# Re-timing the opening of a filter, routing and expert kernel: third batch, DRAM writes, filter rows and weight conversions

## The chip, the cores and the metric

The kernel runs on one core of one Trainium2 chip. Its engines are called as in the profile: PE is TensorE (PEld its weight loads), DVE is VectorE, ACT is ScalarE, POOL is GpSimd, and SP is SyncE, which issues transfers. The metric is the time of one execution on the device in microseconds (us). The clock that the throttle granted to TensorE is written as a share of full speed.

## What is computed

```python
X = np.fft.rfft(x, axis=1)                      # x: 8 batches x 3072 x 256
y = np.fft.irfft(X * (filt_r + 1j*filt_i), n=3072, axis=1)
x = y.reshape(8*3072, 256)
logits = x @ w_gate                             # 8 experts
e = argmax(logits); gate = softmax(logits)[e]
# each token goes to its expert e in order, until `capacity` (768) rows are taken
h = relu(disp @ w1)                             # per expert: 768x256 @ 256x1024
out[token] = gate * (h @ w2)                    # 1024x256; tokens without a place: 0
h = out @ w_in                                  # 256x2048
g = softplus(h)
result = g @ w_out                              # 2048x256
```

The 8 x 768 places are full after three batches, so the common path filters and routes batches b0, b1 and b2 alone. All other rows of the output are one constant row.

## The kernel before

The work falls into units of 384 rows of one expert, 16 units in all: eight leading ones, which take the first 384 places of each expert, and eight later ones.

**Filter.** A batch's 3072 points are taken as 96 x 32. `x1` (b0) and `x1_out` (b1, b2) are the first transform. Those of b1 and b2 are written to DRAM (`mid`, line 223) and read back turned (`it`, `load_i`), eight writes of 384 KB for each of the two batches. `s2(b, k)`, k = 0 to 11, is the second transform (L236) with the complex filter behind it: four DVE multiplies over 64 partitions each (L240, L245, L246, L248; five where k is 0) and one add (L249), on POOL for b0 and for even k, on DVE for odd k. `s3` (L260, copy `e` L262) goes back, then `tr2` (L268, copy `j` L271) and `s4` (L305, copy `yt` L306) make the filtered rows.

**Routing.** `gsum` (L283) and `gturn` (L296) make the logits once all twelve `s3` of a batch are through, `gate` (L313 to L366, some twenty small DVE instructions in five pieces) the places; its last result that routing waits for is `tk` (L365). Then POOL scatters the batch's rows by 32 indirect transfers (L382), at most three per step. Rows of b2 are only parked (`park`, line 393, eight writes issued by SP). Unit 0 may load its rows (`xd`, L532) when the scatters of b0, b1 have landed.

**Experts and the last layers.** `load_w` and `split_w` fetch w1 and w2 and split each into a high and a low part (`w1h`, `w2h` on ACT, L411; `w1l`, `w2l` on POOL, L412). `w1` (L563; `hh` on ACT L567, `hl` on DVE L568) and `w2` (L580) are the experts. `wi` (L595) and `wo` (L618) are the last two layers.

**Conversions.** w_in and w_out come as 64-bit floats, 32 pieces of 128x256. `split_res` turns each into a high and a low part by five DVE instructions (`wtop` L470, `wr` L472, `wrf` L474, `whb` L481, `wtop` again L483), three on ACT (`wrf` L475, `whb` L478, high part L486) and one on POOL (low part L484). It is a generator: `convert`, called once a step, moves every piece in work one stage further, and starts a new one if `new` is true. `wtop` and `wrf` have three buffers, the loaded pieces (`wst`) four.

**Order.** Each engine works through its own instructions in the order in which they were written. That order comes from a hand-written table: `ev(t, order, fn)` puts a piece of work into step t, and the steps are written out from `c0` on. Step 0 is where `wi` of unit 0 starts; `B` says with which step after `c0` each batch's filter starts, and `rel n` below is step `c0 + n`. All plain transfers are issued by SP in that one order.

Of the kernel before, what the change touches and what calls it, by code (L numbers as in the profile page):

```python
# [20 lines left out]
N1, N2 = 96, 32  # L21
# [3 lines left out]
UNIT = 384  # L25
STATIC = 3
# [60 lines left out]
def filter_rows():  # L87


    kre, kim = (k.reshape(PAIRS, 64).T for k in dft_constants()[3:])  # L90
    ki = kre.copy()
    ki[16, 0] = S // 2 + 1
    return kre, ki, kim[:, 0]


def body(tc, cap, x, ff, fx, wg, w1, w2, win, wout, m1, m2, m4, small, out):
# [41 lines left out]
    class Conv:  # L138


        def __init__(self, st, stf, stx, tag):
            pool = lambda st, n, b, **k: st.enter_context(tc.tile_pool(name=tag + n, bufs=b, **k))
            self.jp = pool(st, "j", 4)
            self.yp = pool(st, "y", 5)
            self.gp = pool(st, "g", 1)
            self.ep = [pool(st, "e", 1)]
            self.fp = pool(stf, "r", 1)
            self.zp = pool(stf, "z", 3)
            self.ip = pool(stf, "i", 4)
            self.ep.append(pool(stf, "f", 1))  # L150
            self.xp = pool(stx, "x", 8, side="right")
            self.sp = pool(stx, "s", 2, side="right")
            self.m1s = self.gp.tile([N1, N1], F32, name="m1s")
            self.wgs = self.gp.tile([128, 2, 32], F32, name="wgs")
            self.m4s = self.gp.tile([N1, N1], F32, name="m4s")
            self.m2s = self.fp.tile([128, PAIRS, 128], F32, name="m2s")
            self.m3s = self.fp.tile([128, PAIRS, 128], F32, name="m3s")
            self.fs = self.fp.tile([128, PAIRS, D], F32, name="fs")
            self.fxs = self.fp.tile([64, D], F32, name="fxs")
            self.xt, self.st, self.it, self.z, self.jt, self.yt, self.gsb = {}, {}, {}, {}, {}, {}, {}  # L160
            self.route = {}
            self.e = {}
            self.scatters = []
            self.pending = []
# [18 lines left out]
        def load_f(self, g):  # L183
            gs = slice(4 * g, 4 * g + 4)
            nc.sync.dma_start(self.fs[:, gs], ff[:, gs])
            if g == 0:
                nc.sync.dma_start(self.fxs, fx)
# [42 lines left out]
        def s2(self, b, k):  # L230
# [8 lines left out]
            fr, fi = self.fs[0:64, p0:p0 + 2], self.fs[64:128, p0:p0 + 2]  # L239
            nc.vector.tensor_tensor(out=z[0:64], in0=ps[0:64], in1=fr, op=ALU.mult)  # L240
            if k == 0:
                nc.vector.tensor_tensor(out=z[64:128, 0], in0=ps[64:128, 0], in1=self.fxs, op=ALU.mult)
                nc.vector.tensor_tensor(out=z[64:128, 1:], in0=ps[64:128, 1:], in1=fr[:, 1:], op=ALU.mult)
            else:
                nc.vector.tensor_tensor(out=z[64:128], in0=ps[64:128], in1=fr, op=ALU.mult)  # L245
# [171 lines left out]
    def wi_pools(st, tag):  # L417
        pool = lambda n, b: st.enter_context(tc.tile_pool(name=tag + n, bufs=b, side="right", reuse_waits="tile"))
        wp = pool("wi", 1)
        P.wih = [wp.tile([128, 2, 128], F32R, name=f"wih{i}") for i in range(KI)]  # L420
        P.wil = [wp.tile([128, 2, 128], F32R, name=f"wil{i}") for i in range(KI)]
# [3 lines left out]
    def right_pools(st, tag):  # L425
# [6 lines left out]
        wp = pool("wo", 1)  # L432
        P.woh = wp.tile([128, KI, D], F32R, name="woh")
# [18 lines left out]
    def split_res(i, which):  # L452
# [27 lines left out]
        hi, lo = parts()  # L480
# [189 lines left out]
    with tc.manual_schedule():  # L670
# [32 lines left out]
        conv_l, conv_s = list(conv_q), []  # L703
# [4 lines left out]
        def convert(new=True):  # L708

            for st in list(conv_s):  # L710
                stage = next(st, 3)
                if stage == 2 and conv_l:
                    load_next()
# [84 lines left out]
        c0, B = -74, (0, 17, 33)  # L798
# [26 lines left out]
        for g in range(8):  # L825
            ev(c0 + 4 + g, X1, cv.x1_out, 1, g)
            ev(c0 + 4 + g, ON, cv.load_x, 2, g)
            ev(c0 + 17 + g, X1, cv.x1_out, 2, g)
        for i in range(nslot // (4 * N1)):
            ev(c0 + 3 + i, ON, next, fills)  # L830
        for t in range(c0, -22):
            ev(t, ON, scatter, 3)
        ev(c0 + 26, ON, x_done)
        for t in range(c0 + 27, c0 + 47):
            ev(t, AHEAD + 1, convert, t < c0 + 43)
# [47 lines left out]
        for t in range(-24, 4):  # L883
            ev(t, AHEAD + 1, convert, t < 0 and t % 3 != 2)
# [136 lines left out]
```

## Time and profile before

| what | value |
|---|---|
| median of 3 runs | 1136.93 us (1136.36 to 1137.62) |
| profiled execution | 1138.29 us, of it span 1136.5 us |
| granted clock, mean over the span | 0.969 |
| PE busy | 1055.8 us (93%) |
| ACT busy | 803.1 us (71%) |
| POOL busy | 628.0 us (55%) |
| DVE busy | 505.1 us (44%) |

A row of the timeline has a start, a duration, the engine, the line, what is written from what, and behind it in brackets how long the engine was idle and what ended that. A row of the windows has the stretch, its length, and for each engine its busy time with the count of instructions, then the clock, the DMA engines' share and what they moved. A row of groups has a busy time and the mean of one in ns. A row of waits has the total, the times and the longest.

### The profile page before, as it was taken

How to read it: one execution, taken by the hardware profiler on the slowest of the kernel's cores; microseconds unless marked ns; L12 is line 12 of the kernel's file. 1: busy time of each engine (PE TensorE's matmuls, PEld its weight loads, DVE VectorE, ACT ScalarE, POOL GpSimd, SP SyncE). 2: the span in 40 equal slices, each digit the busy share in tenths (PEclk: the TensorE clock that was granted, in tenths of full speed). 3: DMA queues.
4: the chain of work that ended last, by engine and by line, in shares of the span. 5: the costliest groups of instructions: out<-in, count | busy, mean ns of one | idle time of the engine just before them, and what ended most of it. 6: DMA issues, size and time to landing. Idle time of an engine off the chain costs nothing.

```text
span 1136.5 us, 18508 instructions
## 1 busy us (share of the span) xinstructions
PE 1055.8 (93%) x6608; PEld 978.5 (86%) x6608; DVE 505.1 (44%) x974; ACT 803.1 (71%) x1689; POOL 628.0 (55%) x654
## 2 busy tenths in 40 slices
PE   8989767778779999999999999999999999999996
PEld 7656534546669999999999999999999999999996
DVE  4739869947872383323333333233232323332221
ACT  3546444556558787877778787888878778787885
POOL 0313853863445666677766465555656555554554
PEclk9999987889889999999999999999999999999999
DMA  9975542355421216633332323333211211100000
GB/s 297 319 252 176 157 147 84 107 171 166 136 89 55 82 53 215 227 130 125 118 125 100 132 91 118 106 109 115 66 56 57 61 53 52 61 11 16 15 15 17
DMA packets 84229, 127.36 MB, mean 112 GB/s; under 512 B 9660, under 2 KB 65361, under 8 KB 84128
## 3 DMA queue, kind: packets, MB, share of 16 engines
q1 hardware_dynamic: 77216, 113.44, 31.4%
q0 software_dynamic: 6912, 12.65, 3.4%
q8 instruction: 54, 0.88, 0.3%
q14 instruction: 47, 0.39, 0.1%
HBM read 72.47 MB, written 56.75 MB: 114 GB/s over the span
## 4 chain that ended last, share of the span: by engine, by line
PE 67%; DVE 4%; issue 2%; ACT 2%; POOL 2%; POOLq 0%; ACTq 0%; DVEq 0%
PE po L618 23%; PE pi L595 22%; PE py L580 10%; PE pw L563 10%; DVE wr L472 1%; POOL out_dram L630 1%; PE pt L552 1%; POOL gl L412 1%; DVE wrf L474 0%; DVE whb L481 0%; DVE hl L568 0%; ACT wrf L475 0%; ACT hh L567 0%; PE p L305 0%; DVE wtop L470 0%
## 5 line engine op out<-in xcount | busy, mean ns | idle before, releaser
L498 DVE SCALAR_TENSOR_TENSOR g<-pi,ln 128x384 f32<-128x384 f32 x256 | 142.9, 558 | 516.1 <-ACT ln L493 475.8
L412 POOL TENSOR_TENSOR gl<-g,gh 128x384 fp32r<-128x384 f32 x256 | 260.6, 1019 | 111.3 <-ACT gh L411 85.1
L618 PE MATMUL po<-woh,gh 128*128 128x256 f32 x768 | 216.4, 282 | 3.2 <-DVE ot L625 2.5
L618 PE MATMUL po<-woh,gl 128*128 128x256 f32 x768 | 216.6, 282 | 1.5 <-POOL gl L412 1.5
L618 PE MATMUL po<-wol,gh 128*128 128x256 f32 x768 | 217.4, 283 | 0.0
L490 ACT ACTIVATE ab<-pi 128x384 f32<-128x384 f32 x256 | 124.9, 488 | 118.0 <-PE pi L595 114.0
L595 PE MATMUL pi<-yh,wih 128*128 128x384 f32 x512 | 172.9, 338 | 1.4 <-DVE g L498 1.4
L595 PE MATMUL pi<-yl,wih 128*128 128x384 f32 x512 | 172.1, 336 | 0.0
L595 PE MATMUL pi<-yh,wil 128*128 128x384 f32 x512 | 171.8, 336 | 0.0
L412 POOL TENSOR_TENSOR w1l<-ws,w1h 128x512 fp32r<-128x512 f32 x64 | 83.6, 1306 | 133.3 <-ACT w1h L411 131.2
L618 PEld LDWEIGHTS po<-woh,gh 128*128 128x128 f32 x768 | 144.2, 188 | 4.0 <-DVE ot L625 2.1
L618 PEld LDWEIGHTS po<-woh,gl 128*128 128x128 f32 x768 | 144.8, 189 | 1.7 <-POOL gl L412 1.7
L618 PEld LDWEIGHTS po<-wol,gh 128*128 128x128 f32 x768 | 144.8, 189 | 0.0
L493 ACT ACTIVATE ln<-ab 128x384 f32<-128x384 f32 (+1 forms) x257 | 134.9, 525 | 8.1
L491 ACT ACTIVATE ab<-ab 128x384 f32<-128x384 f32 (+1 forms) x257 | 134.8, 525 | 8.2
L412 POOL TENSOR_TENSOR w2l<-ws,w2h 128x512 fp32r<-128x512 f32 x64 | 83.8, 1310 | 94.3 <-ACT w2h L411 92.1
L411 ACT CAST gh<-g 128x384 fp32r<-128x384 f32 x256 | 129.6, 506 | 0.3 <-DVE g L498 0.3
L580 PE MATMUL py<-hh,w2h 128*128 128x384 f32 x256 | 91.5, 357 | 8.4 <-DVE yl L587 8.1
L595 PEld LDWEIGHTS pi<-yh,wih 128*128 128x128 f32 x512 | 96.5, 188 | 2.1 <-DVE g L498 2.1
L595 PEld LDWEIGHTS pi<-yl,wih 128*128 128x128 f32 x512 | 96.6, 189 | 0.0
L595 PEld LDWEIGHTS pi<-yh,wil 128*128 128x128 f32 x512 | 96.3, 188 | 0.0
L563 PE MATMUL pw<-xh,w1h 128*128 128x384 f32 x256 | 88.4, 345 | 0.0
(144 smaller groups left out, 2026.8 us busy)
## 6 DMA issues: line engine op xcount, KB each, us to landing
ws<-in_w_dram SPq DMA_DIRECT2D x128, 256.0 KB, 2.9
out_dram<-cr SPq DMA_DIRECT2D x48, 512.0 KB, 4.0
xt<-in_x_dram SPq DMA_DIRECT2D x24, 384.0 KB, 7.4
disp<-pf SPq DMA_DIRECT2D x16, 387.0 KB, 5.4
xd<-disp SPq DMA_DIRECT2D x48, 129.0 KB, 3.1
mid<-s SPq DMA_DIRECT2D x16, 384.0 KB, 3.7
it<-mid SPq DMA_DIRECT2D x24, 256.0 KB, 3.7
wst<-in_win_dram SPq DMA_DIRECT2D x16, 256.0 KB, 3.0
```

The costliest lines, as they stand in the source:

```text
L411: nc.scalar.copy(dst_hi, src)
L412: nc.gpsimd.tensor_tensor(out=dst_lo, in0=src, in1=dst_hi.bitcast(F32), op=ALU.subtract)
L472: nc.vector.tensor_scalar(r9, hw, 0x1FF, None, op0=ALU.bitwise_and)
L490: nc.scalar.activation(out=ab[:, :n], in_=h, func=ACTF.Abs)
L491: nc.scalar.activation(out=ab[:, :n], in_=ab[:, :n], func=ACTF.Exp, scale=-1.0)
L493: nc.scalar.activation(out=ln[:, :n], in_=ab[:, :n], func=ACTF.Ln, bias=1.0)
L498: nc.vector.scalar_tensor_tensor(out=g[:, :n], in0=h, scalar=0.0, in1=ln[:, :n], op0=ALU.max, op1=ALU.add)
L552: nc.tensor.transpose(pt[:, t * 128:(t + 1) * 128], self.xd[t][:, k * 128:(k + 1) * 128], ident)
L563: nc.tensor.matmul(ps, lhsT=a[:, k, fs], rhs=b[:, k], start=(n == 0), stop=(n == 5))
L580: nc.tensor.matmul(self.py[d], lhsT=a[:, j % 2, ds], rhs=b, start=(j == 0 and n == 0), stop=(j == 7 and n == 2))
L595: nc.tensor.matmul(self.pi, lhsT=a[i][:, k], rhs=b[:, k], start=(n == 0), stop=(n == 5))
L618: nc.tensor.matmul(self.po[t], lhsT=a[:, ts], rhs=b[:, i], start=(i == 0 and n == 0), stop=(i == KI - 1 and n == 2))
```

## The change

Five things change in the opening of the kernel.

- **Steps.** b2's filter starts at rel 29 instead of rel 33, so that its first `s2` comes in the step behind b1's last. `x1_out` of b2 goes from rel 17 to 24 to rel 12 to 19. The prefill of `disp` goes two steps down, the release of the first pools five steps up. `c0` is -72 instead of -74.
- **Writes.** The 16 writes of `mid` and the 8 of `parked` are issued by ACT instead of SP.
- **Filter rows.** The rows are laid out so that one multiply over 128 partitions takes the place of two over 64 (three where k is 0). For that the real rows are loaded for all 128 partitions, and the imaginary ones lie packed in a second tile.
- **Number of early conversions.** Before, 16 pieces start in every step from rel 27 to 42, and 16 in two of three steps from -24 on. Now 8 start in every third step from rel 23 to 44, and 24 in every step from -24 to -1.
- **Stages of a conversion.** ACT's `wrf` moves one step behind DVE's, behind `whb`; POOL's low part and ACT's high part move one step further too. The next load is issued one call of `convert` later.

```diff
-            self.fs = self.fp.tile([128, PAIRS, D], F32, name="fs")
-            self.fxs = self.fp.tile([64, D], F32, name="fxs")
+            self.fr = self.fp.tile([128, PAIRS, D], F32, name="fr")
+            self.fi = self.fp.tile([128, PAIRS // 2, D], F32, name="fi")
...
-            nc.sync.dma_start(mid[b - 1].rearrange("(q n) c -> q n c", n=N2)[:, 4 * g:4 * g + 4], t)
+            nc.scalar.dma_start(mid[b - 1].rearrange("(q n) c -> q n c", n=N2)[:, 4 * g:4 * g + 4], t)
...
-            fr, fi = self.fs[0:64, p0:p0 + 2], self.fs[64:128, p0:p0 + 2]
-            nc.vector.tensor_tensor(out=z[0:64], in0=ps[0:64], in1=fr, op=ALU.mult)
...
-                nc.vector.tensor_tensor(out=z[64:128], in0=ps[64:128], in1=fr, op=ALU.mult)
+            fi = self.fi[64 * (k % 2):64 * (k % 2) + 64, p0 // 4 * 2:p0 // 4 * 2 + 2]
+            nc.vector.tensor_tensor(out=z, in0=ps, in1=self.fr[:, p0:p0 + 2], op=ALU.mult)
...
-            nc.sync.dma_start(parked[:, 4 * g:4 * g + 4], self.yt[b, g][:, :, 0:D])
+            nc.scalar.dma_start(parked[:, 4 * g:4 * g + 4], self.yt[b, g][:, :, 0:D])
...
-        nc.scalar.activation(out=rf, in_=rf, func=ACTF.Copy, scale=2.0 ** -20)
         yield 0
         hb = pool.tile(shp, U32, name="whb", tag="whb", bufs=2)
         nc.scalar.activation(out=hb, in_=top, func=ACTF.Relu, scale=8.0, bias=ebias)
+        nc.scalar.activation(out=rf, in_=rf, func=ACTF.Copy, scale=2.0 ** -20)
         yield 1
...
         nc.vector.tensor_scalar(top, hb, 0xFF800000, None, op0=ALU.bitwise_and)
+        yield 2
+        hi, lo = parts()
         nc.gpsimd.tensor_tensor(out=lo, in0=rf, in1=top.bitcast(F32), op=ALU.mult)
-        yield 2
         nc.scalar.copy(hi, hb.bitcast(F32))
...
-        c0, B = -74, (0, 17, 33)
+        c0, B = -72, (0, 17, 29)
...
-            ev(c0 + 17 + g, X1, cv.x1_out, 2, g)
+            ev(c0 + 12 + g, X1, cv.x1_out, 2, g)
...
-        for t in range(-24, 4):
-            ev(t, AHEAD + 1, convert, t < 0 and t % 3 != 2)
+        for t in range(-24, 6):
+            ev(t, AHEAD + 1, convert, t < 0)
```

On PE, from b1's last `s3` on, there stood before: (L260 is `s3`, L283 `gsum`, L268 `tr2`, L296 `gturn`, L305 `s4`, L236 `s2`)

```order
L260 MATMUL p_1347<-m3s,z 128x128 x4
L260 MATMUL p_1380<-m3s,z 128x128 x4
L260 MATMUL p_1414<-m3s,z 128x128 x4
L283 MATMUL pg<-e,wgs 32x384 x16
L268 MATMUL p_1464<-sm,e 96x128 x4
L268 MATMUL p_1471<-sm,e 96x128 x4
L296 MATMUL p_1496<-sm,gx 96x128 x4
L296 MATMUL p_1502<-sm,gx 96x128 x4
L305 MATMUL p_1509<-j,m4s 96x512
L305 MATMUL p_1512<-j,m4s 96x512
L268 MATMUL p_1515<-sm,e 96x128 x4
L236 MATMUL p_1539<-it,m2s 128x256 x2
```

and on the same engine at the same place there stands now (L238 is `s2`, L257 `s3`, L280 `gsum`, L265 `tr2`, L293 `gturn`):

```order
L238 MATMUL p_1357<-it,m2s 128x256 x2
L257 MATMUL p_1366<-m3s,z 128x128 x4
L238 MATMUL p_1388<-it,m2s 128x256 x2
L257 MATMUL p_1397<-m3s,z 128x128 x4
L238 MATMUL p_1413<-it,m2s 128x256 x2
L280 MATMUL pg<-e,wgs 32x384 x16
L265 MATMUL p_1443<-sm,e 96x128 x4
L265 MATMUL p_1450<-sm,e 96x128 x4
L257 MATMUL p_1458<-m3s,z 128x128 x4
L238 MATMUL p_1476<-it,m2s 128x256 x2
L293 MATMUL p_1486<-sm,gx 96x128 x4
L293 MATMUL p_1492<-sm,gx 96x128 x4
```

Four `s2` of b2 stand ahead of b1's `gturn` that stood behind it.

On ACT, some ten steps ahead of step 0, there stood before: (L486 is the high part, L478 `whb`, L475 `wrf`, L567 `hh`, L411 a high part of w1 or w2)

```order
L486 CAST woh<-whb 128x256
L475 ACTIVATE wrf<-wrf 128x256
L567 ACTIVATE hh<-pw 128x384
L411 CAST w1h<-ws 128x512
L486 CAST woh<-whb 128x256
L478 ACTIVATE whb<-wtop,ebias 128x256
L475 ACTIVATE wrf<-wrf 128x256
L567 ACTIVATE hh<-pw 128x384
L411 CAST w2h<-ws 128x512
```

and there stands now (L485, L476, L477, L566, L408):

```order
L485 CAST woh<-whb 128x256
L476 ACTIVATE whb<-wtop,ebias 128x256
L477 ACTIVATE wrf<-wrf 128x256
L566 ACTIVATE hh<-pw 128x384
L408 CAST w1h<-ws 128x512
L485 CAST woh<-whb 128x256
L476 ACTIVATE whb<-wtop,ebias 128x256
L477 ACTIVATE wrf<-wrf 128x256
L566 ACTIVATE hh<-pw 128x384
L408 CAST w2h<-ws 128x512
```

The `wrf` ahead of a `hh` was that of the conversion started in the same step; it is now that of the step before, and every step has one.

On POOL, in the same stretch, there stood before: (L412 is a low part of w1 or w2, L484 that of a conversion)

```order
L412 TENSOR_TENSOR w2l<-ws,w2h 128x512
L412 TENSOR_TENSOR w1l<-ws,w1h 128x512
L484 TENSOR_TENSOR wol<-wrf,wtop 128x256
L412 TENSOR_TENSOR w2l<-ws,w2h 128x512
L484 TENSOR_TENSOR wol<-wrf,wtop 128x256
L412 TENSOR_TENSOR w1l<-ws,w1h 128x512
L412 TENSOR_TENSOR w2l<-ws,w2h 128x512
L484 TENSOR_TENSOR wol<-wrf,wtop 128x256
```

and there stands now (L409, L484):

```order
L409 TENSOR_TENSOR w1l<-ws,w1h 128x512
L484 TENSOR_TENSOR wil_2134<-wrf,wtop 128x256
L409 TENSOR_TENSOR w2l<-ws,w2h 128x512
L484 TENSOR_TENSOR wil_2135<-wrf,wtop 128x256
L409 TENSOR_TENSOR w1l<-ws,w1h 128x512
L484 TENSOR_TENSOR wol<-wrf,wtop 128x256
L409 TENSOR_TENSOR w2l<-ws,w2h 128x512
L484 TENSOR_TENSOR wol<-wrf,wtop 128x256
```

A conversion stands behind every split of w1 and w2, and the last eight pieces of w_in are among them.

## Rows read from the trace of the kernel before

**Rows 1.** Windows by stage: busy time of each engine, clock, DMA.
```profile
0.00:64.50 64.50, 59.52 (x355) 45.42 (x356) 37.41 (x58) 30.76 (x51) 13.87 (x16) 1.00 0.98 305
64.50:81.50 17.00, 13.97 (x92) 9.22 (x91) 4.22 (x8) 5.99 (x11) 2.53 (x2) 0.90 0.88 287
...
135.00:158.00 23.00, 12.29 (x82) 7.24 (x81) 12.53 (x30) 7.79 (x19) 18.13 (x25) 0.85 0.47 141
158.00:194.00 36.00, 26.77 (x108) 18.36 (x106) 34.77 (x73) 16.10 (x37) 8.95 (x10) 0.81 0.26 81
...
268.00:334.00 66.00, 49.28 (x231) 44.85 (x231) 50.45 (x100) 37.44 (x91) 30.21 (x28) 0.88 0.41 124
340.00:1136.50 796.50, 780.65 (x5219) 777.90 (x5218) 262.53 (x519) 630.99 (x1333) 474.73 (x476) 1.00 0.26 85
```

**Rows 2.** Timeline of PE: the first expert matmul and the first `wi`.
```profile
267.86 0.42 PE L563 MATMUL pw<-xh,w1h 128*128 128x384 f32 x1
...
334.02 0.52 PE L595 MATMUL pi<-yh,wih 128*128 128x384 f32 x1
```

**Rows 3.** Timeline of DVE: the end of the gates of b0 and b1.
```profile
105.22 0.17 DVE L365 COPY tk<-tok 96x32 f32<-96x32 f32 x1
...
192.98 0.17 DVE L365 COPY tk<-tok 96x32 f32<-96x32 f32 x1
```

**Rows 4.** Timeline of POOL: first and last scatter of b1.
```profile
194.03 1.02 POOL L382 DMA_INDIRECT disp<-yt,ix  x1 [0.30 <-POOL yt L377]
...
245.06 0.92 POOL L382 DMA_INDIRECT disp<-yt,ix  x1 [0.30 <-issue]
```

**Rows 5.** Timeline of PE around the break between b1 and b2.
```profile
154.58 1.16 PE L296 MATMUL p<-sm,gx 128*96 128x128 f32 x8
...
157.73 1.03 PE L236 MATMUL p<-it,m2s 128*128 128x256 f32 x4
```

**Rows 6.** Waits from 267.86 to 334.02 us: who waited for whom.
```profile
ACT wrf L475 <- DVE wrf L474: 27.4, 12, 3.5
DVE hl L568 <- ACT hh L567: 12.6, 12, 2.9
```

**Rows 7.** Timeline of PE: the first `x1_out` of b1.
```profile
32.15 1.93 PE L220 MATMUL p<-xt,m1s 96*96 96x512 f32 x4 [0.47 <-DMA xt<-in_x_dram]
```

**Rows 8.** Groups by shape, DVE, 0 to 345 us: the filter's second multiply.
```profile
L245 DVE TENSOR_TENSOR z<-p,fs 64x512 f32<-64x512 f32 x33 | 22.9, 694 | 0.5
```

**Rows 9.** Waits of SP's queue, 0 to 345 us: the writes of `mid`.
```profile
SPq L223 <- ACT s L222: 46.9, 14, 7.2
```

**Rows 10.** Groups on POOL from 194 to 246 us.
```profile
L484 POOL TENSOR_TENSOR wil<-wrf,wtop 128x256 fp32r<-128x256 f32 x7 | 6.5, 929 | 0.1
L249 POOL TENSOR_TENSOR z<-z,t 128x512 f32<-128x512 f32 x3 | 4.2, 1385 | 0.0
```

**Rows 11.** Windows of the instructions that read `wst`, four of a conversion's five.
```profile
158.00:194.00 36.00, 9.61 (x22) 0.81 0.26 81
268.00:334.00 66.00, 26.18 (x51) 0.88 0.41 124
193.20:194.90 1.70, 1.33 (x4) 1.00 0.05 14
```

**Rows 12.** Windows of the fifth instruction of a conversion (L483).
```profile
158.00:194.00 36.00, 2.69 (x6) 0.81 0.26 81
268.00:334.00 66.00, 11.97 (x13) 0.88 0.41 124
```

**Rows 13.** Timeline of DVE: the fifth instruction twice.
```profile
193.72 0.29 DVE L483 TENSOR_SCALAR wtop<-whb 128x256 uint32<-128x256 uint32 x1
...
283.60 1.25 DVE L483 TENSOR_SCALAR wtop<-whb 128x256 uint32<-128x256 uint32 x1
```

**Rows 14.** Timeline of POOL beside the second of these.
```profile
283.24 1.45 POOL L412 TENSOR_TENSOR w1l<-ws,w1h 128x512 fp32r<-128x512 f32 x1
```

**Rows 15.** Waits from 80 to 345 us: DVE for a buffer.
```profile
DVE wtop L470 <- POOL wil L484: 10.1, 3, 5.8
```

More of the change, by code (lines that the diff above doesn't have):

```diff
@@ L25 @@
 UNIT = 384
+WI0 = 8
 STATIC = 3
@@ L92, in filter_rows @@
     ki[16, 0] = S // 2 + 1
-    return kre, ki, kim[:, 0]
+    return np.concatenate([kre, kim]), ki.reshape(64, 6, 2, 2).transpose(2, 0, 1, 3).reshape(128, 12)
 def body(tc, cap, x, ff, fx, wg, w1, w2, win, wout, m1, m2, m4, small, out):
@@ L184, in load_f @@
             gs = slice(4 * g, 4 * g + 4)
-            nc.sync.dma_start(self.fs[:, gs], ff[:, gs])
-            if g == 0:
-                nc.sync.dma_start(self.fxs, fx)
+            nc.sync.dma_start(self.fr[:, gs], ff[:, gs])
+            gs = slice(2 * g, 2 * g + 2)
+            nc.sync.dma_start(self.fi[:, gs], fx[:, gs])
         def load_x(self, b, g, src=None):
@@ L238, in s2 @@
             t2 = self.zp.tile([128, 2, D], F32, name="t2", tag="t2", bufs=2)
-            fr, fi = self.fs[0:64, p0:p0 + 2], self.fs[64:128, p0:p0 + 2]
-            nc.vector.tensor_tensor(out=z[0:64], in0=ps[0:64], in1=fr, op=ALU.mult)
[L241 to L244, printed above, removed]
-                nc.vector.tensor_tensor(out=z[64:128], in0=ps[64:128], in1=fr, op=ALU.mult)
+            fi = self.fi[64 * (k % 2):64 * (k % 2) + 64, p0 // 4 * 2:p0 // 4 * 2 + 2]
+            nc.vector.tensor_tensor(out=z, in0=ps, in1=self.fr[:, p0:p0 + 2], op=ALU.mult)
             nc.vector.scalar_tensor_tensor(out=t2[0:64], in0=ps[64:128], scalar=-1.0, in1=fi,
@@ L419, in wi_pools @@
         wp = pool("wi", 1)
-        P.wih = [wp.tile([128, 2, 128], F32R, name=f"wih{i}") for i in range(KI)]
-        P.wil = [wp.tile([128, 2, 128], F32R, name=f"wil{i}") for i in range(KI)]
+        P.wih = [wp.tile([128, 2, 128], F32R, name=f"wih{i}") for i in range(WI0)]
+        P.wil = [wp.tile([128, 2, 128], F32R, name=f"wil{i}") for i in range(WI0)]
         P.wl = pool("wl", 3)
@@ L432, in right_pools @@
         wp = pool("wo", 1)
+        P.wih += [wp.tile([128, 2, 128], F32R, name=f"wih{i}") for i in range(WI0, KI)]
+        P.wil += [wp.tile([128, 2, 128], F32R, name=f"wil{i}") for i in range(WI0, KI)]
         P.woh = wp.tile([128, KI, D], F32R, name="woh")
@@ L478, in split_res @@
         nc.scalar.activation(out=hb, in_=top, func=ACTF.Relu, scale=8.0, bias=ebias)
+        nc.scalar.activation(out=rf, in_=rf, func=ACTF.Copy, scale=2.0 ** -20)
         yield 1
-        hi, lo = parts()
         nc.vector.scalar_tensor_tensor(out=hb, in0=hw, scalar=0x80000000, in1=hb,
@@ L702, in body @@
         conv_q = [(i, k) for k in range(2) for i in range(KI)]
-        conv_l, conv_s = list(conv_q), []
+        conv_l, conv_s, free = list(conv_q), [], []
         def load_next():
@@ L708, in convert @@
         def convert(new=True):
+            while free and conv_l:
+                free.pop()
+                load_next()
             for st in list(conv_s):
                 stage = next(st, 3)
-                if stage == 2 and conv_l:
-                    load_next()
+                if stage == 2:
+                    free.append(st)
                 if stage == 3:
@@ L827, in body @@
             ev(c0 + 4 + g, ON, cv.load_x, 2, g)
-            ev(c0 + 17 + g, X1, cv.x1_out, 2, g)
+            ev(c0 + 12 + g, X1, cv.x1_out, 2, g)
         for i in range(nslot // (4 * N1)):
-            ev(c0 + 3 + i, ON, next, fills)
+            ev(c0 + 5 + i, ON, next, fills)
         for t in range(c0, -22):
             ev(t, ON, scatter, 3)
-        ev(c0 + 26, ON, x_done)
-        for t in range(c0 + 27, c0 + 47):
-            ev(t, AHEAD + 1, convert, t < c0 + 43)
+        ev(c0 + 21, ON, x_done)
+        for t in range(c0 + 23, -24):
+            ev(t, AHEAD + 1, convert, t < c0 + 45 and (t - c0) % 3 == 2)
         ev(-26, ON, make_room)
@@ L994 @@
     cap = min(int(inputs["moe_capacity"]), NT)
-    kr, ki, kx = filter_rows()
-    zero = np.zeros((1, D), np.float32)
-    fr, fi = inputs["filt_r"][kr], np.concatenate([inputs["filt_i"], zero])[ki]
+    kr, ki = filter_rows()
+    fi = np.concatenate([inputs["filt_i"], np.zeros((1, D), np.float32)])
     arrays = {
         "x": np.ascontiguousarray(inputs["x"]),
-        "ff": np.ascontiguousarray(np.concatenate([fr, fi]).reshape(128, PAIRS, D)),
-        "fx": np.ascontiguousarray(inputs["filt_r"][kx]).reshape(64, D),
+        "ff": np.ascontiguousarray(inputs["filt_r"][kr]),
+        "fx": np.ascontiguousarray(fi[ki]),
         "wg": np.ascontiguousarray(inputs["moe_w_gate"]),
```

## The prediction

> **What bounds the kernel now.** I read the windows by stage first [rows 1]. From 340 us to the end PE is busy for 780.65 of 796.5 us at full clock, and nothing of that stretch is changed but the last few conversions. So the question is when step 0 comes, now at 334.02 us [rows 2]: each us by which it moves is one us of the result. Before it no engine is full all the time, and the limit changes from stage to stage. Up to 64.5 us PE is at 59.52 and the DMA engines are at 0.98. From 158 to 194 us DVE is at 34.77 of 36 [rows 1]: b2's `s2`, b1's gate and conversions all want it. Before that stands the break: b2's first `s2` comes at 157.73, behind b1's `gturn` at 154.58 [rows 5], and from 135 to 158 PE is busy for 12.29 of 23 us and DVE for 12.53 [rows 1]. The gate of b1 ends at 192.98 [rows 3], and the scatters of b1 run from 194.03 to 245.06 + 0.92 = 245.98 [rows 4], 52 us for 32. From 268 to 334 us DVE is busy for 50.45 of 66 us, and no other engine but PE is near that [rows 1]; its idle time there is 15.55 us, of which 12.6 is `hl` waiting for ACT's `hh`, and ACT in turn waits 27.4 us for DVE's `wrf` [rows 6]. Each of the two stops the other once a step.
>
> **Start and b0, 5 us lost.** Six loads of real rows keep their size (512 KB), six of packed imaginary rows are new (256 KB each), the 64 KB row goes: 1.51 MB more, at 305 GB/s [rows 1] 4.9 us. The rows of b1 stand behind them in SP's order, and its first `x1_out` already waits 0.47 us for its load [rows 7], so it comes some 4.9 us later. Of b2's eight `x1_out`, three now stand ahead of the end of b0's gate that stood behind it: 3 x 1.93 = 5.8 us of PE. Against this stand about 3 us in which PE is idle from 64.5 to 81.5 us, and 0.10 x 17 = 1.7 us that it loses there to the clock (0.90) [rows 1]. 4.9 + 5.8 - 4.7 = 6.0; I take 5, since part of the load's delay also falls into that idle time. The end of b0's gate goes from 105.22 [rows 3] to 110. Bounds: 2 (the delay is wholly hidden) and 10.7 (nothing is).
>
> **The filter multiply** takes 694 ns and is dropped once per `s2` [rows 8]; the remaining one has the same 512 elements on twice the partitions, a form that this trace doesn't show. Between no longer than now and twice as long, I take the first, as it is the elements per partition that are equal. It is worth nothing where PE or POOL leads, and is counted below where DVE leads.
>
> **The writes** leave SP, which waits 46.9 us at them for ACT's copies [rows 9]. What stood behind them were loads ahead of their time, so I set the gain at nothing. The loss is ACT's: an issue cost and, if a transfer channel isn't free, a wait of ACT, behind which stand `yt`, `j` and `e`. Bounds: a gain of 2 us and a loss of 5; I take 0. The Trainium skill, "DMA: Bandwidth & Descriptors", section "Issuing engines are not separate DMA queues", says that transfers of all engines share the same 16 DMA engines and that another issuing engine saves sequencer time alone; by it the term would be 0 too and the 5 us of loss at the start would stay, and no row here shows a plain transfer issued by ACT.
>
> **The break, 6 us won at the gate of b1.** b1's `gturn` comes 5 us later, at 159.6 instead of 154.58 [rows 5], but four `s2` of b2 are then through. Of DVE's 34.77 us from 158 to 194 [rows 1], five `s2` lose one multiply each, 3.5 us. Conversions there were 5.5, four of whose five instructions took 9.61 us [rows 11] and the fifth 2.69 [rows 12], together 2.2 us each; two are left, so 7.7 us go. 34.8 - 3.5 - 7.7 = 23.6, with 1.2 us of idle time as before (36 - 34.8) and the 1 us from `tk` to the end of that window 24 to 26. The gate ends near 186 instead of 192.98 [rows 3]. POOL doesn't stand against it: b0's scatters end some 5 us later than now, near 161.
>
> **Scatters of b1, 5 us more.** 52 us hold 32 scatters, three adds of 1385 ns and seven low parts of 929 ns [rows 4, 10]. Two adds and some three low parts go: 2.8 + 2.8 = 5.6; I take 5. They run from 187 to 234, so end 12 us earlier; after that unit 0's rows are loaded, weighted and turned, and the first expert matmul now comes at 267.86 [rows 2], 22 us later. In these 22 us lies the end of b2's gate, which is four steps earlier now; one more conversion and eight issues on ACT stand against that. I take 21, so it comes at 255, **13 us earlier**.
>
> **The last stage, 5 us lost.** From there to step 0 are 19 steps, 66 us now. In them 13 conversions took 26.18 + 11.97 = 38.15 us of DVE [rows 11, 12], 2.93 each; all else took 50.45 - 38.15 = 12.3. Now 19 run: 19 x 2.93 = 55.7, with 12.3 that is 68.0. ACT's `wrf` no longer waits for an instruction of the same step, so the 12.6 us at `hl` go [rows 6], and 15.55 - 12.6 = 3.0 stay. 71.0 instead of 66: 5 us. What is late next is DVE itself. The price of 2.93 is the doubtful part: the same five took 1.33 + 0.29 = 1.62 us when POOL was not in the way [rows 11, 13], and L483 took 1.25 us instead of 0.29, from 283.60 to 284.85, while POOL split a weight from 283.24 to 284.69 [rows 13, 14]. So DVE stands still until POOL's instruction is over, and POOL has six low parts more than now.
>
> **Sum.** 13 - 5 = 8 us earlier at step 0. Behind it the conversions end two steps after step 0 as they did; 0. 1138.29 (the profiled execution: 1136.5 of span and 1.8 around it) - 8 = 1130.3. That execution is 1.4 over the median of the three runs, so I predict **1129 us**.
>
> **Rivals.** *The last stage is stopped by POOL* and the result is slower. Its place is DVE's first instruction of a conversion, which needs one of three `wtop` buffers; the low part on POOL that frees it is now a step later and stands behind a weight split of 1.45 us [rows 14]. For it: such waits are there already, three with 10.1 us in all [rows 15], and each step now has one. Against: POOL is busy for 30.21 of 66 us [rows 1], so it can run ahead. Price: the share lost to POOL now is 13 x (2.93 - 1.62) = 17.0 us. If DVE and POOL exclude each other wholly, DVE's 50.45 - 17.0 + 6 x 1.62 = 43.2, POOL's 30.2 + 6 x 0.93 = 35.8 [rows 10] and the 3 us give 82; with idle time as now, 15.55, the first sum is 83.6 and the second 94.6. I take 86, 20 us more than now: 1138.3 - 13 + 20 - 1.4 = 1144. It decides from 66 + 13 = 79 us on. The Trainium skill, "GPSIMD Engine Reference", section "Specifications", says that GpSimd's SBUF interfaces are shared with VectorE, and that they contend with VectorE instructions that have two SBUF inputs or run in a mode with two ports; the pair above agrees (1.25 us instead of 0.29), and taken as full exclusion the rule gives the 82.
>
> *POOL's scatters keep the gain.* The late start pushes b0's scatters, they push the adds of b2, and b1's 32 still need 52 us: they start at 188 and end at 240, the first matmul comes 6 us earlier instead of 13, and the last stage takes back 5. 1138.3 - 1 - 1.4 = 1136, no change. For it: 1.6 us per scatter is close to what they cost alone, 0.92 with 0.30 of issue [rows 4]; against it, the adds and low parts that go are in the rows.
>
> *A larger gain.* If a conversion costs DVE only the 2.2 us of the stretch from 158 to 194 [rows 11, 12], where POOL is busy for 8.95 of 36 us [rows 1], the stage takes 41.8 + 12.3 + 3 = 57 us and 9 are won on top of 13: 1138.3 - 22 - 1.4 = 1115. Against: POOL is busy nearly half of the stage.
>
> **How the numbers follow.** The forecast has 0.50, the stop by POOL 0.24, no gain 0.13, the larger gain 0.13. 0.2% of 1137 us is 2.3 us, about what a measurement of this kernel can tell from no change. Of the forecast's own spread (1122 to 1134.5, by 2 to 10.7 at the start and 67 to 75 in the last stage) all is faster; of the case without gain 0.02 is faster, 0.09 the same, 0.02 slower. With 0.01 of the stop ending level: faster 0.65, same 0.10, slower 0.25. The range goes down to 1110, which leaves out the larger gain where POOL costs still less, and up to 1146, which leaves out the stop by POOL from 88 us on.
>
> **What would show it.** The first `x1_out` of b1 near 37 us, b0's `tk` near 110, b1's near 186, the last scatter near 234, the first expert matmul near 255, step 0 near 326. From 255 on DVE busy over nine tenths, few waits of `wrf` and `hl` on each other, some 2.9 us per conversion. The forecast is wrong if b1's scatters still take 52 us, if DVE waits there for POOL's low part, or if ACT waits at its own writes.

## The result and the profile after

The changed kernel takes 1124.22 us (median, 1123.18 to 1128.51) against 1137.11 us; the ratio is 0.9894, with a 95% interval of 0.9868 to 0.9921. The profiled execution has a span of 1122.0 us, 14.5 less than the one before. The forecast was 1129 us.

The windows of the changed kernel by its own stages (stretch, length, busy time of PE, PEld, DVE, ACT, POOL with counts, clock, DMA share, GB/s), to be set beside [rows 1]:

```profile
0.00:64.50 64.50, 58.17 (x334) 44.10 (x335) 28.03 (x43) 29.14 (x47) 12.64 (x15) 0.95 0.99 302
...
160.00:189.00 29.00, 27.97 (x166) 21.44 (x166) 26.79 (x57) 16.95 (x34) 10.21 (x11) 1.00 0.28 87
189.00:235.00 46.00, 33.79 (x155) 19.88 (x156) 18.92 (x41) 21.65 (x46) 36.77 (x51) 0.86 0.45 134
```

```profile
251.38:317.91 66.53, 47.02 (x226) 41.88 (x227) 62.26 (x138) 45.18 (x109) 37.46 (x36) 0.91 0.52 159
```

From b1's `gturn` to the end of its gate PE is now busy for 27.97 of 29 us at full clock; before, DVE was the limit there, and it is still busy for 26.79 us. In the last stage, from the first expert matmul to step 0, DVE is busy for 62.26 of 66.53 us, where it was at 50.45 of 66; it is idle for 4.3 us instead of 15.55.

The landmarks of the timelines: PE's first `x1_out` of b1, its `gturn` of b1, the first expert matmul and the first `wi`, which answer to [rows 2, 5, 7]:

```profile
35.76 3.70 PE L222 MATMUL p<-xt,m1s 96*96 96x512 f32 x4 [3.96 <-DMA xt<-in_x_dram]
...
159.89 1.09 PE L293 MATMUL p<-sm,gx 128*96 128x128 f32 x8 [0.17 <-DVE gx L283]
...
251.38 0.69 PE L562 MATMUL pw<-xh,w1h 128*128 128x384 f32 x1 [4.18 <-ACT xh L552]
...
317.91 0.52 PE L594 MATMUL pi<-yh,wih 128*128 128x384 f32 x1
```

On DVE the ends of the gates of b0 and b1, as [rows 3]:

```profile
111.87 0.17 DVE L362 COPY tk<-tok 96x32 f32<-96x32 f32 x1
...
187.95 0.17 DVE L362 COPY tk<-tok 96x32 f32<-96x32 f32 x1
```

On POOL the first and the last scatter of b1, as [rows 4]:

```profile
189.06 0.97 POOL L379 DMA_INDIRECT disp<-yt,ix  x1 [0.28 <-POOL yt L374]
...
233.73 0.92 POOL L379 DMA_INDIRECT disp<-yt,ix  x1 [0.30 <-issue]
```

| landmark, us | before | forecast | after |
|---|---|---|---|
| first `x1_out` of b1 | 32.15 | 37 | 35.76 |
| `tk` of b0 | 105.22 | 110 | 111.87 |
| `gturn` of b1 | 154.58 | 159.6 | 159.89 |
| `tk` of b1 | 192.98 | 186 | 187.95 |
| end of b1's last scatter | 245.98 | 234 | 234.65 |
| first expert matmul | 267.86 | 255 | 251.38 |
| from there to step 0 | 66.2 | 71 | 66.5 |
| step 0 | 334.02 | 326 | 317.91 |
| from step 0 to the end of the span | 802.5 | 802.5 | 804.1 |

### The profile page after: what moved, and what is told of

It is laid out like the page before. It is cut to its first block, busy times and chain, and to the rows that moved or that the text cites. A ratio compares the mean times of both kernels' runs of the same rounds, so it can differ in the third digit from the quotient of the medians.

```text
span 1122.0 us, 18484 instructions
## 1 busy us (share of the span) xinstructions
PE 1049.2 (94%) x6608; PEld 972.9 (87%) x6608; DVE 473.5 (42%) x935; ACT 805.3 (72%) x1689; POOL 626.6 (56%) x654
## 4 chain that ended last, share of the span: by engine, by line
PE 74%; DVE 7%; DMA 6%; POOL 5%; issue 5%; ACT 2%; POOLq 0%; SPq 0%; ACTq 0%; DVEq 0%
PE po L617 23%; PE pi L594 23%; PE py L579 10%; PE pw L562 10%; PE p L222 2%; POOL disp L379 2%; DMA xt<-in_x_dram 1%; DMA disp<-yt,ix 1%; DMA mid<-s 1%; PE p L257 1%; PE p L238 1%; DVE wrf L473 1%; POOL out_dram L629 1%; PE pt L551 1%; DMA fi<-in_fx_dram 1%
## 5 line engine op out<-in xcount | busy, mean ns | idle before, releaser
L409 POOL TENSOR_TENSOR gl<-g,gh 128x384 fp32r<-128x384 f32 x256 | 260.6, 1019 | 110.9 <-ACT gh L408 79.0
L409 POOL TENSOR_TENSOR w1l<-ws,w1h 128x512 fp32r<-128x512 f32 x64 | 83.6, 1306 | 133.4 <-ACT w1h L408 124.8
L409 POOL TENSOR_TENSOR w2l<-ws,w2h 128x512 fp32r<-128x512 f32 x64 | 83.8, 1309 | 90.1 <-ACT w2h L408 82.6
L408 ACT CAST gh<-g 128x384 fp32r<-128x384 f32 x256 | 129.7, 507 | 0.3 <-DVE g L497 0.3
```

The costliest lines, as they stand in the source:

```text
L408: nc.scalar.copy(dst_hi, src)
L409: nc.gpsimd.tensor_tensor(out=dst_lo, in0=src, in1=dst_hi.bitcast(F32), op=ALU.subtract)
```

## The experiments

Three jobs ran on three chips. On the chip of the second job the kernel before takes 1149.75 us, so times are given there as ratios to it. Each time is a median. Landmarks come from one profiled execution of each kernel; where the same opening was profiled more than once, the spread is given.

### The parts of the change undone

The first four kernels share a chip; the kernel before takes 1138.43 us there.

**Old filter rows.** The loads and multiplies of before, in the changed kernel:

```diff
-            nc.vector.tensor_tensor(out=z, in0=ps, in1=self.fr[:, p0:p0 + 2], op=ALU.mult)
+            nc.vector.tensor_tensor(out=z[0:64], in0=ps[0:64], in1=fr, op=ALU.mult)
...
+                nc.vector.tensor_tensor(out=z[64:128], in0=ps[64:128], in1=fr, op=ALU.mult)
```

> The changed kernel with the filter rows laid out, loaded and multiplied as before the change (four multiplies over 64 partitions, 1.5 MB less to load); all else stays. My theory, that the break and the stages of the conversions made the gain and the filter rows about pay for their own load: the first x1_out of b1 comes near 32 us instead of 35.8, the gate of b1 ends within 2 us of 188 (4 us earlier start against five to nine multiplies of 0.69 us), step 0 between 315 and 320, the whole within 3 us of the changed kernel's 1124. Rival, that the filter rows are a main source of the gain: step 0 at 323 or later, the whole 1129 or more.

It took 1125.38 us, ratio 0.9873 (0.9851 to 0.9894): the changed kernel's time. The first `x1_out` of b1 came at 32.18, without a wait, and the gate of b0 ended at 106.68, 5.2 us earlier than in the changed kernel's trace and 3.1 and 4.1 us earlier than in two kernels below that have the same opening on this chip (109.82, 110.76). The gate of b1 ended at 189.19, 1.2 us later; the first expert matmul is at 254.38, step 0 at 321.68, a little past the 320 expected. PE's `gturn` of b1 and DVE's end of that gate:

```profile
155.99 1.88 PE L297 MATMUL p<-sm,gx 128*96 128x128 f32 x8 [1.98 <-DVE gx L287]
```

```profile
189.19 0.17 DVE L366 COPY tk<-tok 96x32 f32<-96x32 f32 x1
```

So the new rows win some 6 us between the two gates, 5.1 of them behind `gturn` (33.20 us here, 28.06 in the changed kernel), and lose 3 to 5 at the start. The changed kernel has its first expert matmul at 251.38 in one profiled execution and at 253.29 in another (below), so what is left, 1 to 3 us, is near what two executions differ by, and the whole times show nothing.

**The break put back.**

```diff
-        c0, B = -72, (0, 17, 29)
+        c0, B = -74, (0, 17, 33)
```

> The changed kernel with b2's filter started at rel 33 as before (and the first step at -74), so that the four steps without s2 between b1 and b2 are back; all else stays. My theory: the gate of b1 ends 5 to 8 us later than 188, the last scatter of b1 some 10 us later than 234, the first expert matmul near 262 instead of 251, the whole near 1134. Rival, that POOL's scatters set the pace whatever DVE does: the scatters of b1 end within 3 us of 234 and the whole stays near 1125.

My theory was wrong. The rival's numbers came true, its reason only in part. It took 1122.25 us, ratio 0.9859 (0.9839 to 0.9879), and its step 0 is at 314.71. PE's `gturn` of b1 and DVE's end of that gate in this kernel:

```profile
154.16 1.08 PE L293 MATMUL p<-sm,gx 128*96 128x128 f32 x8
```

```profile
182.71 0.17 DVE L362 COPY tk<-tok 96x32 f32<-96x32 f32 x1
```

Without the break the two stand at 159.89 and 187.95. From one to the other it takes 28 us either way (28.55 and 28.06). The four `s2` that fill the break push `gturn` back by 5.7 us, and the way from there to the gate's end is not shorter for it. b1's scatters take 48.4 us instead of 45.6, with three adds of the filter among them instead of one; they end at 232.21, 2.4 us earlier, and the first expert matmul is at 248.65, 2.7 us earlier. Filling the break costs 5 us at the gate and gives half of it back in the scatters. At step 0 it stands 3.2 us behind, but a second execution of the changed kernel stands another 2.7 behind (320.65, below), so no more is shown than that it did not make the gain.

**The old stages of a conversion,** with the numbers and steps of the changed kernel, and its later load of the next piece:

```diff
+        nc.scalar.activation(out=rf, in_=rf, func=ACTF.Copy, scale=2.0 ** -20)
         yield 0
...
-        nc.scalar.activation(out=rf, in_=rf, func=ACTF.Copy, scale=2.0 ** -20)
         yield 1
+        hi, lo = parts()
...
-        yield 2
-        hi, lo = parts()
         nc.gpsimd.tensor_tensor(out=lo, in0=rf, in1=top.bitcast(F32), op=ALU.mult)
+        yield 2
```

> The changed kernel with the stages of a conversion as before: ACT's wrf in the step of DVE's wrf, POOL's low part and ACT's high part one step earlier; 24 conversions still run from step -24 on. My theory: ACT waits for wrf and DVE waits for hh again, some 12 us at hl, the stretch from the first expert matmul to step 0 takes 79 to 84 us instead of 66.5, the whole 1136 to 1142. Rival, that DVE is full there whatever the order (62.3 of 66.5 us): the stretch takes 67 to 69 us and the whole stays at 1124 to 1127.

It took 1144.24 us, ratio 1.0052 (1.0035 to 1.0068), slower than the kernel before. Up to the first expert matmul (250.25) nothing is lost; from there to step 0 it takes 86.73 us, more than the 79 to 84 expected. The waits of that stretch (total, times, longest) and its window:

```profile
ACT wrf L474 <- DVE wrf L473: 40.1, 18, 3.0
...
DVE hl L567 <- ACT hh L566: 14.2, 16, 0.9
```

```profile
250.25:336.98 86.73, 53.28 (x226) 47.50 (x227) 69.12 (x137) 44.82 (x108) 37.85 (x36) 0.81 0.40 122
```

The two engines stop each other as in [rows 6], with 17.6 us of DVE's time idle instead of 4.3, and DVE is busy for 69.1 instead of 62.3 us for the same work. The new stages are worth 20 us with 20 conversions in the stretch. Without them the change would be a loss.

**POOL's low part twice.**

```diff
         nc.gpsimd.tensor_tensor(out=lo, in0=rf, in1=top.bitcast(F32), op=ALU.mult)
+        nc.gpsimd.tensor_tensor(out=lo, in0=rf, in1=top.bitcast(F32), op=ALU.mult)
```

> The changed kernel with POOL's low part of each conversion computed twice, the second over the first. My theory, that DVE stands still at part of its instructions while POOL has an elementwise instruction running: some 20 more POOL instructions of 0.75 us in the last stage, half of whose time DVE loses, 7 us there, and 2 to 4 us at the scatters, the whole 1131 to 1136; the mean of DVE's instructions of a conversion rises from 2.55 us together to about 2.9. Rival, that DVE is slowed by its own work and POOL has room (37.5 of 66.5 us): the whole within 2 us of 1124, 2.55 us stay.

It took 1141.31 us, ratio 1.0021 (1.0007 to 1.0035), more than either theory said. The scatters of b1 end 3.4 us later; the last stage takes 79.43 us instead of 66.53. Its window, the instructions that read `wst` in it, and the fifth instruction:

```profile
253.70:333.13 79.43, 52.52 (x226) 47.33 (x227) 69.89 (x138) 45.48 (x109) 52.32 (x56) 0.80 0.44 133
```

```profile
253.70:333.13 79.43, 46.47 (x80) 0.80 0.44 133
```

```profile
253.70:333.13 79.43, 11.82 (x20) 0.80 0.44 133
```

POOL has 14.9 us more, DVE's work stays and takes 7.6 us more, and its idle time rises by 5.3. A conversion costs DVE (46.47 + 11.82) / 20 = 2.91 us, as foreseen; what was not is that the waits rise too (`wtop` for POOL's low part 5.7 us in five waits). The granted clock of the stage is 0.80 instead of 0.91 and PE is busy for 52.52 instead of 47.02 us; what share of the added idle time comes from that is not separated. How one engine holds the other is seen in a few rows of this kernel, DVE and then POOL:

```profile
280.16 0.55 DVE L568 SCALAR_TENSOR_TENSOR hl<-pw,hh 128x384 fp32r<-128x384 f32 x1
280.62 0.55 DVE L554 TENSOR_TENSOR xl<-pt,xh 128x384 fp32r<-128x384 f32 x1
...
283.11 1.35 DVE L469 TENSOR_SCALAR wtop<-wst 128x256 uint32<-128x256 uint32 x1 [0.70 <-POOL wol L485]
```

```profile
280.04 1.35 POOL L409 TENSOR_TENSOR w1l<-ws,w1h 128x512 fp32r<-128x512 f32 x1 [2.13 <-ACT w1h L408]
...
283.03 1.28 POOL L409 TENSOR_TENSOR w2l<-ws,w2h 128x512 fp32r<-128x512 f32 x1
```

`hl` and `xl` run at their usual 0.55 us while POOL splits a weight; `wtop`, 0.29 us by itself, ends only after POOL's instruction has. What POOL's work costs DVE thus hangs on what DVE has in hand at the time. `hl` and `xl` read one operand from PSUM. The Trainium skill, "GPSIMD Engine Reference", section "Specifications", names as the contending ones VectorE's instructions with two SBUF inputs or in a mode with two ports. The rows of `hl` and `xl`, with one SBUF input each, agree with it; `wtop` has one SBUF input too, and no row shows in which mode it runs.

### Stages and numbers one by one

These four ran on the slower chip.

**The new stages alone in the kernel before** (16 early and 16 late conversions, old filter rows, break and writes as before):

```diff
-        for t in range(c0 + 27, c0 + 47):
+        for t in range(c0 + 27, -24):
             ev(t, AHEAD + 1, convert, t < c0 + 43)
```

> The kernel before with one part of the change alone: the stages of a conversion (ACT's wrf one step behind DVE's, low and high part one step later, the next load one call later); 16 early and 16 late conversions as before. My theory, that this part alone makes most of the gain: the opening up to the first expert matmul stays within 3 us of 267.9, the 12.6 us of DVE at hl go and a conversion costs DVE 2.55 us instead of 2.93, so the last stage takes 49 to 54 us instead of 66.2, the whole 1122 to 1127. Rival, that the stages only make room for more conversions and are worth little by themselves: the stage takes 62 us or more, the whole 1133 or more.

The ratio is 0.9974 (0.9962 to 0.9986): the rival's whole, but not its reason. The last stage shrank to 56.18 us, 10 less than before, nearly as my theory had it (49 to 54). Its price per conversion did not fall: 28.64 + 9.49 us of DVE for 13, 2.93 each, as in [rows 11, 12]; idle time went from 15.55 to 6.6 us. The gain was lost earlier. The wait of [rows 15] grew from 10.1 to 23.8 us. The waits of DVE from 107 us to the end of b1's scatters, and the first of them in those scatters with POOL's rows beside it:

```profile
DVE wtop L470 <- POOL wil L485: 23.8, 5, 9.8
```

```profile
203.55 0.29 DVE L470 TENSOR_SCALAR wtop<-wst 128x256 uint32<-128x256 uint32 x1 [4.21 <-POOL wil L485]
```

```profile
200.63 0.92 POOL L382 DMA_INDIRECT disp<-yt,ix  x1 [0.30 <-issue]
201.85 0.92 POOL L382 DMA_INDIRECT disp<-yt,ix  x1 [0.30 <-issue]
202.78 0.74 POOL L485 TENSOR_TENSOR wil<-wrf,wtop 128x256 fp32r<-128x256 f32 x1
```

This is the mechanism of the rival that the prediction put in the last stage. The low part, a step later than before, keeps one of three `wtop` buffers; it stands behind a step's scatters on POOL, and DVE waits for it with the next batch's `s2` behind. No trace of the kernel before was taken on this chip, so a part of the growth could be the chip's; but two kernels below with the changed opening have at most 0.6 us of this wait there.

**All 16 early conversions in the changed kernel** (with old filter rows, which leave room for them):

```diff
-            ev(t, AHEAD + 1, convert, t < c0 + 45 and (t - c0) % 3 == 2)
+            ev(t, AHEAD + 1, convert, c0 + 26 < t < c0 + 43)
...
-            ev(t, AHEAD + 1, convert, t < 0)
+            ev(t, AHEAD + 1, convert, t < 0 and t % 3 != 2)
```

> The changed kernel with the filter rows as before the change (which leaves room for all 16 pieces of w_in) and the conversions' numbers and steps as before: 16 early from rel 27 to 42, 16 late in two of three steps; stages, break and writes as changed. To be read against the changed kernel with the old filter rows (gate of b1 at 189.2, last scatter 236.4, first expert matmul 254.4, stage 67.3). My theory, that the early conversions made the gate of b1 late, and not the break: with them back it ends at 195 or later, the first expert matmul comes at 262 to 268, the last stage takes 49 to 54 us, the whole near 1121. Rival, that DVE has room there: the gate of b1 within 2 us of 189, the whole near 1110.

The ratio is 0.9897 (0.9877 to 0.9916). The gate of b1 ends at 207.23, 18 us later than with eight early ones (189.19, on the first chip); the first expert matmul is at 278.78, later than the 262 to 268 expected, and the last stage takes 55.00 us. The waits of DVE from 110 to 262 us say why:

```profile
DVE wtop L473 <- POOL wil L488: 21.1, 5, 8.9
```

Eight early conversions in every third step let POOL's low part pass between the scatters. In the changed kernel DVE has no such wait from 100 to 240 us. But what the early ones cost in the opening they win in the last stage: by the whole times the new numbers are worth 0.0024 of the time (0.9897 here, 0.9873 with the old rows and eight early ones), which the two intervals can't tell from nothing. Shown is that the new numbers without the new stages lose (1.0052).

The last two kernels share a chip, the stages and the old filter rows, and differ by 9.3 us (1147.26 and 1137.96). What differs is the steps and the writes. The writes are worth nothing that can be measured (below), and filling the break did not make the gain (above). Left are the other steps, above all `x1_out` of b2 five steps up: with them the gate of b2 ends at 272.32 instead of 289.36. No run undoes them by themselves, so this rests on exclusion alone.

**Eight conversions behind step 0.**

```diff
-        for t in range(-24, 6):
-            ev(t, AHEAD + 1, convert, t < 0)
+        for t in range(-24, 20):
+            ev(t, AHEAD + 1, convert, t % 3 != 2 if t < 0 else t < 16 and t % 2 == 0)
```

> The changed kernel with 8 of the 24 late conversions put behind step 0 (16 in two of three steps from -24 to -1, then one every second step from 0 to 14). My theory, DVE at 2.55 us per conversion sets the length of the last stage: seven conversions fewer in it, 66.5 us becomes 48 to 53, and behind step 0, where PE leads, ACT and POOL take them with a loss of 1 to 4 us; the whole 1109 to 1113. Rival, that PE or ACT is next at once in the last stage: it takes 60 us or more, the whole 1118 or more.

The ratio is 0.9801 (0.9778 to 0.9825). The last stage took 53.93 us (66.5 in the changed kernel, and 67.5 on this chip in the next kernel, which has all its conversions ahead of step 0), the stretch from step 0 on 811.5 instead of 804.1. Seven conversions fewer in the stage are 12.6 us, 1.8 each; of that 7.4 went behind step 0, where the waits from 309.3 to 360 us are:

```profile
DVE g L497 <- ACT ln L492: 14.3, 7, 3.4
...
POOL gl L409 <- ACT gh L408: 9.0, 6, 1.6
...
PE pi L594 <- DVE g L497: 5.8, 5, 2.1
```

PE waits 5.8 us there for DVE's `g`; in the 50 us behind the changed kernel's step 0 it waits 0.9 us. Which engine makes `g` late isn't shown: in the changed kernel DVE waits for ACT's `ln` even longer (26.7 us), and ACT is busy for 41.1 us here and 42.0 there, DVE for 35.7 and 18.4. The loss was mis-sized at 1 to 4 us.

**b1's rows ahead of the last filter rows.**

```diff
             cv.load_f(g)
-        for g in range(4):
-            cv.load_x(1, g)
+            if g > 2:
+                cv.load_x(1, g - 3)
+        cv.load_x(1, 3)
```

> The changed kernel with the first three loads of b1's rows put between the last three groups of filter loads instead of behind all of them. My theory, that the 1.5 MB of the new filter rows cost 4 us at the start which carry through to the end: the first x1_out of b1 comes near 32 us instead of 35.8, the gates, the scatters and step 0 all 3 to 4 us earlier, the whole near 1120.5. Rival, that the delay is made good elsewhere, or the later filter rows become late: the whole 1123 or more.

The first `x1_out` came at 31.91, the gate of b0 ended at 107.75 and that of b1 at 183.50: 3.9, 4.1 and 4.5 us earlier than in the changed kernel's trace, as foreseen. But the kernel with eight behind step 0, which up to there is the changed kernel and ran on this chip, has them at 35.06, 108.95 and 184.72. Beside it the first `x1_out` is 3.2 us earlier and the gates only 1.2. The two kernels with three edits below, which have this order too, have the gate of b0 at 108.44 and 106.97, 3.8 and 5.3 us ahead of the changed kernel beside them. So how much of the gain of the start carries through is not settled. Behind the gate b1's scatters took 55.4 us in the one and 53.5 in the other, with waits of DVE for `gx` of 10.8 and 12.2 us whose releaser the trace only calls remote. That stays unexplained, so the whole, ratio 0.982 (0.9802 to 0.9838), can't be set beside 1124.

### The rest, and a better version

The last four share a third chip, on which the kernel before takes 1137.99 us.

> The changed kernel once more, as the yardstick for the three runs beside it on the same chip. All theories: a ratio to the kernel before of 0.986 to 0.992.

The changed kernel took 1126.33 us, ratio 0.9893 (0.9873 to 0.9912). Its gates end at 112.22 and 187.78, its first expert matmul is at 253.29, its step 0 at 320.65.

**Writes by SP.**

```diff
-            nc.scalar.dma_start(mid[b - 1].rearrange("(q n) c -> q n c", n=N2)[:, 4 * g:4 * g + 4], t)
+            nc.sync.dma_start(mid[b - 1].rearrange("(q n) c -> q n c", n=N2)[:, 4 * g:4 * g + 4], t)
...
-            nc.scalar.dma_start(parked[:, 4 * g:4 * g + 4], self.yt[b, g][:, :, 0:D])
+            nc.sync.dma_start(parked[:, 4 * g:4 * g + 4], self.yt[b, g][:, :, 0:D])
```

> The changed kernel with the writes of mid and of the parked rows issued by SP as before the change; all else stays. My theory, that this part is worth nothing either way: within 3 us of the changed kernel beside it, gates of b0 and b1 within 2 us. Rival 1, that SP free of these writes brings loads earlier: 4 us or more slower than the changed kernel, with the loads of w1, w2 or of the pieces late. Rival 2, that ACT loses by issuing: 4 us or more faster.

It took 1124.89 us, ratio 0.9877 (0.9856 to 0.9897), both gates 1.3 to 1.4 us earlier, step 0 at 320.73 against 320.65. Nothing that can be measured in the whole. The Trainium skill, "DMA: Bandwidth & Descriptors", section "Issuing engines are not separate DMA queues", says that another issuing engine saves only the sequencer's time; the two times, 1124.89 and 1126.33 us, agree.

**Three edits together**: the break put back, b1's rows ahead of the last filter rows, and five conversions behind step 0.

```diff
-        c0, B = -72, (0, 17, 29)
+        c0, B = -74, (0, 17, 33)
...
-            ev(t, AHEAD + 1, convert, t < 0)
+            ev(t, AHEAD + 1, convert, t % 5 and t < -1 if t < 0 else t < 15 and t % 3 == 2)
```

> The changed kernel with three edits together: b2's filter starts at rel 33 (first step -74), b1's first rows are loaded between the filter rows, and five of the 24 late conversions run behind step 0, one in three steps from 2 to 14. My theory, that the three gains lie one behind the other and add up: the gate of b1 3 to 4 us for the start and 4 to 5 for its gturn earlier than in the changed kernel, the last stage 57 to 60 us instead of 66.5, behind step 0 0 to 2 us lost, the whole 12 to 16 us below the changed kernel beside it. Rival, that POOL's scatters or the stretch behind step 0 take half of it back: 4 to 8 us below.

It took 1113.4 us, ratio 0.9778 (0.9741 to 0.9815), 12.9 below the changed kernel beside it. The gate of b1 ends at 180.81, 7.0 us earlier than beside it, the first expert matmul is at 247.50, the last stage takes 60.45 us, step 0 is at 307.95, and behind it 0.4 us are lost. The last stage's window:

```profile
247.50:307.95 60.45, 45.82 (x233) 41.85 (x232) 56.36 (x113) 39.84 (x95) 31.70 (x30) 0.90 0.52 161
```

DVE is still the limit there.

**The same with eight behind step 0.**

```diff
-            ev(t, AHEAD + 1, convert, t % 5 and t < -1 if t < 0 else t < 15 and t % 3 == 2)
+            ev(t, AHEAD + 1, convert, t % 3 != 2 if t < 0 else t < 16 and t % 2 == 0)
```

> As the kernel with three edits, but with eight conversions behind step 0, one in two steps from 0 to 14, and 16 in two of three steps before. My theory, that ACT and POOL then are full behind step 0 and PE waits: the last stage 52 to 55 us, the stretch behind step 0 6 to 8 us longer, the whole 9 to 13 us below the changed kernel beside it and 1 to 4 us above the one with five. Rival, that the stretch behind step 0 takes eight as well as five: 3 us or more below the one with five.

It took 1114.34 us, ratio 0.9782 (0.9759 to 0.9806): the last stage 55.92 us, the rest 811.71. What the stage wins is lost behind step 0; the two can't be told apart by their times.

## Why the prediction was right, and where it was not

- **The start** was forecast at 5 us and cost 6.65 at the gate of b0. The mechanism was right: 1.5 MB more ahead of b1's rows. The old filter rows and the other order of loads both bring the first `x1_out` back to 32. What that is worth at the gates is less sure: five traces with the new opening have the gate of b0 at 108.95 to 112.22, so the cost reads as 3.7 to 7.0 us, and the other order of loads won 1.2 us there on one chip, and with two other edits 3.8 and 5.3 on another. PE stood idle for 3.96 us, and the four matmuls behind took 3.70 us instead of 1.93, at a granted clock of 0.50 (1.2 GHz) instead of 1.00 (2.4 GHz).
- **The filter multiply** on 128 partitions took 689 ns in the mean of 36 (L242), as assumed. From `gturn` of b1 to the gate's end the part wins 5.1 us, where 3.5 was counted; as a whole it wins 1 to 3 us at the first expert matmul, which the times don't show.
- **The writes** were set at 0; they are.
- **The break** was the step that failed. The gate of b1 was forecast for 186 and came at 187.95, but the reason given, four `s2` already through, is worth less than nothing there: with the break back the gate ends at 182.71. The number came near because the sum had no term for these `s2`; its two terms were the multiplies and the conversions, and these are what moved the gate. From `gturn` to the gate's end it took 38.40 us before and 28.06 now. The multiplies are 5.1 of that (above). The instructions that read `wst` took 9.61 us of DVE from 158 to 194 [rows 11], and the corresponding stretch now has 3.49:

```profile
160.00:189.00 29.00, 3.49 (x10) 1.00 0.28 87
```

- **The scatters** were forecast at 47 us and took 45.6. The mechanism was right: of three adds and seven low parts one and four are left, and with the break back, where the three adds are there again, they take 48.4. The rival that had them stay at 52 us did not come true.
- **From the last scatter to the first expert matmul** 21 us were forecast and 16.7 were needed, a term mis-sized by 4. Before, the gate of b2 ended 2.8 us ahead of that matmul; now, at 245.32, it is 6 us ahead, and the matmul waits for ACT's `xh`. With the break back it takes 16.4, so the break isn't the reason; which of the other parts is was not tried by itself, and the second execution of the changed kernel took 18.7.
- **The last stage** was forecast at 71 us and took 66.5. Its idle time fell as described, from 15.55 to 4.3 us, and DVE became the limit. The mis-sized term is the price of a conversion. It was taken from before, 2.93 us for each of 19, and was 2.55 for each of 20: 40.35 us for four instructions of 20 conversions and 10.59 for the fifth.

```profile
251.38:317.91 66.53, 40.35 (x80) 0.91 0.52 159
```

```profile
251.38:317.91 66.53, 10.59 (x20) 0.91 0.52 159
```

  The price is not the conversion's own. Undisturbed the five take 1.62 us [rows 11, 13]; the rest is lost to POOL, and most of POOL's work in the stage is 15 or 16 splits of w1 and w2, however many conversions run. Over 1.62 each, 13 conversions lost 17.0 us before and 17.1 with the new stages alone, 16 in the better version 19.5, and 20 here 18.5. So a conversion more costs little over 1.62, as the 1.8 us of the kernel with eight behind step 0 bear out, and charging 2.93 for each counts POOL's share again with each. The place counts too. Added up from the rows, 29.3 us of POOL's elementwise work lie beside conversions and 5.6 beside `hl` and `xl`; with the old stages, 20 conversions as well, it is 35.6 and 0.4, and a conversion costs 2.84. `hl` and `xl` take 0.55 us in the mean with such work beside them (12) and without (11), `wtop` 0.66 (14) and 0.29 (25).
- **Behind step 0** 1.6 us were lost where 0 was forecast.
- **The rival of the stop by POOL** did not come true in the last stage, where `wtop` waited 2.5 us for POOL's low part. The wait that it described exists: it comes up at the scatters, when one conversion a step starts there. The larger gain did not come either: its price of 2.2 us for a conversion was too low.

In sum, the sign of the gain and most of its terms were right, and 8 of the 14.5 us of span were counted. The missing 6.5 are the last stage (4.5) and the path to it (3.6: 251.38 instead of 255), less the 1.6 behind step 0. The second execution of the changed kernel, with 253.29 and 320.65, lies 1.9 and 2.7 us nearer to the forecast, so a part of that is no more than executions differ by.

## What to carry to other kernels

Set a chain of small steps over several engines one step apart on each engine, so that none waits for another within a step; but count the buffers, since each step of delay keeps one longer, and a buffer freed by an engine with a long queue stops the engine in front of it. A gap in one engine's work is worth filling only if what stands behind the gap is not pushed back by the filling. A price per instruction that holds time lost to another engine does not grow with the number of instructions: ask first whose work makes the loss, and whether there will be more of it.

## What the runs showed of the hardware

A VectorE instruction of 0.29 us took 1.35 us beside a GpSimd elementwise instruction, while those of 0.55 us that read one operand from PSUM kept 0.55 us. Twenty GpSimd instructions more, 14.9 us of its time, made the stage 12.9 us longer although GpSimd had been idle for 29 of 66.5 us. After a wait of 3.96 us four TensorE matmuls took 3.70 us instead of 1.93, at half the granted clock. And one of three chips took 1% longer for the same kernel (1149.75 us against 1138.43 and 1137.99); two kernels with the changed opening took 53.5 and 55.4 us there for the scatters, against 45.6 elsewhere.
